# A new order of the first key, query and weight units in an attention-and-Mish kernel planned by hand

## The chip, the cores and the metric

The kernel runs on one core of one Trainium2 chip. The metric is the device time of one execution in microseconds. Before the change it is 1046.02 us, the median of three runs (1045.72 to 1046.89).

## The reference, cut to what matters

Two blocks follow each other, all in float32. The first is a linear attention with random features, for 8 batches, 8 heads, 576 positions and 64 dimensions per head:

```python
def phi(x):
    proj = np.einsum('bhsd,df->bhsf', x, w_phi)
    proj = proj - np.max(np.abs(proj), axis=-1, keepdims=True)
    return np.concatenate([np.exp(proj), np.exp(-proj)], axis=-1)
q_p, k_p = (phi(q), phi(k))
kv = np.einsum('bhsf,bhsd->bhfd', k_p, v)
z = np.sum(k_p, axis=2)
num = np.einsum('bhsf,bhfd->bhsd', q_p, kv)
den = np.einsum('bhsf,bhf->bhs', q_p, z)[..., None] + 1e-06
return (num / den).astype(np.float32)
```

The second takes the result as 4608 tokens of 512 numbers: `h = x @ w_in` (512 to 2048), `g = h * tanh(softplus(h))` (Mish), `g @ w_out` (2048 to 512).

## The kernel before, in words

Everything is cut into tasks. A class `Plan` receives each task with an engine, a key, an estimated duration, what it depends on and which buffers it takes and gives back. `Plan.order` walks through a modelled time: whenever an engine is free, it takes the ready task with the lowest key. The result is one fixed list, and on the chip each engine (TensorE or PE, VectorE or DVE, ScalarE or ACT, and SyncE or SP for DMA) works through its part of that list strictly in order. Keys are thus priorities, not times; a key that changes moves tasks in the queues of all four engines.

**Key units.** A key unit k0 to k35 is 512 positions of two heads each. `load_raw` (L352) fetches 256 KB; `project` (L360) multiplies by `w_phi` into two PSUM banks; `centre_max` (L364) takes the largest absolute value of each row on DVE, and `centre` (L372) subtracts it, also on DVE; `k_exp` (L436, L437) takes both exponentials on ACT, four activations of 128x512 for a unit; `k_sum` (L401) multiplies them with the values v (`load_v`, L431, 330 KB for a pair of heads). A pair of heads spans 4.5 tiles of 128 positions, so a sum runs over two units: k0 holds the first four tiles of pair 0, k1 the last one and four of pair 1, and so on. When a pair is complete, `kv_copy` takes its sum out of PSUM, on ACT (L469) if the pair is in `KVACT`, else on DVE (L471).

**Units in `BYACT`** take another way: DVE only finds the maximum (L392) and its negative (L395), and ACT computes the exponentials straight from PSUM with the maximum as its bias (L386), 16 activations of 128x128 in place of four of 128x512. Before the change these are k3 and k8.

**Query units.** q0_0, q0_1, q1_0, q1_1, q2_0, q2_1 are the first six (numbers 0 to 5 in `FIRST_QUERIES`): chunk c of 256 tokens, half g of the heads. They are projected and centred in the same way, turned by PE (`dt`, L480), go through ACT (L490), are multiplied with the sums (`num`, L401), divided on DVE (L523 to L525), turned again (`xt`, L545) and split into a high and a low part (`xTh` on ACT, L553; `xTl` on DVE, L559). A unit with g = 0 needs the sums of pairs 0 and 1, a unit with g = 1 those of pairs 2 and 3; pair 3 ends in k4.

**Weight units.** `w_in` and `w_out` lie in HBM as float64; 32 pieces of 512 KB each (in_0 to in_3 come first) are loaded as words (L251), most of them a second time shifted by two bytes ("middle", also L251), and turned into a high and a low float32 part by ACT (L265, L326) and six steps on DVE (L279, L284, L292, L297, L302, L307). There are three homes for middles, so the fourth middle waits until the first piece is split. `WKEYS` holds the keys of the 32 pieces.

**The second block.** The first matmuls of `h` (L575) need both halves of chunk 0 and the pieces in_0 to in_3; after that, `h` and `o` (L610) and, from chunk 4 on, a form with fewer products (L745) fill PE up to the end.

The order around the change is set by `FIRST_KEYS` and `FIRST_QUERIES` (the priority t of each early unit) and `WKEYS`. The priority of a load follows from t:

```python
load = (-40.0 + t if t < -3 else -46.6 + 0.2 * t) if first else t - 4.0
```

The words of weight piece i are loaded with key -47.5 + 0.1 i, its middle with -47.45 + 0.1 i. Of the first 11 loads in the list, those of v are moved back by about 4.5 places; four weight loads are moved behind the load of v5. All DMAs go through SP's one queue.

Of the kernel before, what the change touches and what calls it, by code (L numbers as in the profile page):

```python
# [33 lines left out]
PAIRED = 0  # L34
PSTEP = 1.0
NFLIGHT = 4
BYACT = (3, 8,)
KVACT = (0, 2, 3, 5, 6, 7,)
SLACK = -0.137
LAGF = 6  # L40
NMIX = 3
# [13 lines left out]

NK, LEAD = B * NHP * S // 512, 5
LEADIN = 5
FIRST_KEYS = {0: -15.83, 1: -13.11, 2: -9.97, 3: -9.13, 4: -7.79, 5: 5.39, 6: 7.33, 7: 10.36, 8: 12.26, 9: 26.17, 10: 26.27}
FIRST_QUERIES = {0: -11.55, 1: -8.5, 2: -1.4, 3: -0.74, 4: 12.74, 5: 12.11}
NFIRST = 6  # L60
NTRIAL = 3
NLOADS = 11
# [5 lines left out]
E1 = 0.171  # L68
GX = 0.403
ET = 0.107  # L70
WKEYS = [-6.42, -8.84, -5.8, -0.77, 4.55, 2.54, 6.13, 9.34, 4.27, 5.56, 11.66, 11.19, 18.21, 21.9, 23.26, 22.05,
         25.09, 22.07, 26.7, 34.84, 24.54, 37.47, 32.85, 40.81, 37.93, 41.3, 40.78, 41.2, 43.66, 37.64, 39.51, 45.36]
LAG, TAIL, TAILLAG = 4, 10, 2
TWOH = 10
HFIRST = 0.0
# [123 lines left out]
def attention_then_mish(ctx, tc, qT, kT, va, w_phi, w_in, w_out, out):  # L199
# [239 lines left out]
    def parts_of_unit(n):  # L439

        found = {}
        for i in range(4):
            for p, slot in pairs_of(4 * n + i):
                found.setdefault(p, []).append((i, slot))
        return found
# [16 lines left out]
    def kv_copy(p, more):  # L462
# [4 lines left out]
        kv[p // NHP, p % NHP] = work.tile([P, 2, 2, VW], F32, tag="kv", name=f"kv_{p}", bufs=NKV)  # L467
        if p in KVACT:
            nc.scalar.copy(kv[p // NHP, p % NHP], ps)  # L469
# [342 lines left out]
    add = plan.add  # L812
    key_time = dict(FIRST_KEYS)
    query_time = dict(FIRST_QUERIES)
    for n in range(NFIRST, 2 * NCH):
# [4 lines left out]
    def unit_tasks(unit, step, t, load, src, kinds, size):  # L820
# [12 lines left out]
        when = t - UCENTRE * (step >= NFIRST)  # L833
        if unit[0] == "k" and int(unit[1:]) in BYACT:
            add(f"centre {unit} 0", "DVE", t, 1.4, lambda: both_maxima(unit), deps=[f"project {unit}"])
# [23 lines left out]
    for t, is_query, n in units:  # L859
# [5 lines left out]
        if not is_query:  # L865
            unit = f"k{n}"
            kinds = ("h", "att") if n >= LEAD + TWOH else ("att", "att") if n % 2 or n >= LEADIN else ("h", "h")
            unit_tasks(unit, n - LEAD, t + 0.01 * steady, load, kT[n], kinds, 262144)
            for j in range(2):
                if n in BYACT:  # L870
                    home = e_homes_of[unit][j]
                    add(f"exp {unit} {j}", "ACT", exps[j], 1.75, lambda unit=unit, j=j, home=home: centred_exp(unit, j, home),
                        deps=[f"centre {unit} 0"], after=[f"exp {unit} 0"] if j else [], take=[(home, f"e{j}:{unit}")],
# [3 lines left out]
            mine = list(parts_of_unit(n).items())  # L877
            for k, (p, parts) in enumerate(mine):
                deps, take, give = [f"exp {unit} 0", f"exp {unit} 1"], [], []
                split, begins, ends, last = p >= SPLIT_PAIR, parts[0][1] == 0, parts[-1][1] == 4, k == len(mine) - 1  # L880
                bank_kind = "o" if p < NHP else "att"
                vslot = spare[NRAWSPARE // 2 + p] if p < NHP else "v"
                if begins:
                    add(f"load v{p}", "SP", load + 0.3, 0.42, lambda p=p: load_v(p), take=[(vslot, f"v:{p}")], size=337920,
                        after=turned_at(n - LEAD - 1))
                    deps.append(f"load v{p}")
                if begins or split:
                    take.append((bank_kind, f"kvps:{p}:{n if split else 0}"))
                if ends:
                    last_use.setdefault(vslot, []).append(f"sum {unit} {p}")  # L890
                    give.append(f"v:{p}")
                if last:
                    for h in e_homes_of[unit]:
                        last_use.setdefault(h, []).append(f"sum {unit} {p}")
                    give += [f"e{j}:{unit}" for j in range(2)]
                if steady:
                    sums_at.setdefault(n - LEAD, []).append(f"sum {unit} {p}")
                add(f"sum {unit} {p}", "PE", sums, 0.05 + 0.466 * len(parts), lambda n=n, p=p, last=last: k_sum(n, p, last),
                    deps=deps, after=[f"sum {unit} {mine[k - 1][0]}"] if k else [],
                    near=[f"exp q{(n - LEAD) // 2}_{(n - LEAD) % 2} {j}" for j in range(2)] if steady and n >= LEAD + 2 * NTURNED else [], take=take, give=give)  # L900
                if ends or split:
                    more = split and not begins
                    add(f"kv {p}" if ends else f"kv {p} first", "ACT" if p in KVACT else "DVE", sums + 0.01 - URGENT * steady, 0.34, lambda p=p, more=more: kv_copy(p, more),
                        deps=[f"sum {unit} {p}"] + ([f"kv {p} first"] if more else []), take=[] if more else [("kv", f"kv:{p}")],
                        give=[f"kvps:{p}:{n if split else 0}"])
        else:
            c, g = divmod(n, 2)
            unit = f"q{c}_{g}"
# [3 lines left out]
            for j in range(2):  # L912
                if by_dma:
# [6 lines left out]
                        deps=[f"turn {unit} {j}"], table="exp")  # L920
# [8 lines left out]
            for i in range(2):  # L929
                pair = 2 * g + i  # L930
                if steady:
                    sums_at.setdefault(n if is_query else n - LEAD, []).append(f"num {unit} {i}")
                add(f"num {unit} {i}", "PE", sums + 0.01, 0.95, lambda c=c, g=g, i=i: q_num(c, g, i),
                    deps=[f"exp {unit} 0", f"exp {unit} 1"] + [f"kv {b * NHP + pair}" for b in batches],
# [3 lines left out]
                    deps=[f"num {unit} {i}"], after=[f"divide {unit} 0"] if i else [], take=[] if i else [("half", f"x:{unit}")], give=[f"num{i}:{unit}"])  # L938
            outs = sums + GX if steady else t + 1.2
            if by_dma:  # L940
                add(f"regroup {unit}", "DVE", sums + 0.1, 0.68, lambda c=c, g=g: x_regroup(c, g),
                    deps=[f"divide {unit} {i}" for i in range(2)], take=[("part", f"via:{unit}")])
# [12 lines left out]
    for i, pc in enumerate(pieces):  # L955
# [4 lines left out]
            deps=last_use.get(slot, []) + used, after=ahead, take=[(slot, f"w:{nm}")], size=524288)  # L960
        if i < nmiddle:
            home = homes[i % len(homes)]
            add(f"middle {nm}", "SP", -47.45 + i * 0.1, 0.42, lambda pc=pc, home=home: load_middle(*pc, home),
                deps=last_use.get(home, []), take=[(home, f"m:{nm}")], size=524288)
        add(f"abs {nm}", "ACT", WKEYS[i] - 0.5, 0.55, lambda pc=pc: magnitude(*pc), deps=[f"load {nm}"], take=[("w", f"u:{nm}"), ("part", f"w:{nm}")])
        def split(step, took, fn, deps, **more):
            add(f"{step} {nm}", "DVE", WKEYS[i], took, lambda pc=pc, fn=fn: fn(pc), deps=deps, late=0.13, **more)

# [99 lines left out]
    for m in range(NFT // 2):  # L1068
        t = PREP + PSTEP * m
        for k in range(2):  # L1070
            add(f"wsum {m} {k}", "DVE", t, 0.61, lambda m=m, k=k: w_sum(m, k),
                deps=[f"{s} {('out', 2 * m + k, 0)}" for s in ("ready", "split")] + ([] if k else PREP_DEPS),
                after=[f"wsum {m} 0"] if k else [],
                take=[] if k else [("part", f"wsum0:{m}"), ("part", f"wsum1:{m}"), ("prep", f"prep:{m}")])
        for which in range(3):
# [3 lines left out]
                deps=[f"wsum {m} {k}" for k in range(2)], after=[f"comb {m} {which - 1}"] if which else [],  # L1079
# [3 lines left out]
                deps=[f"comb {m} {which}"])  # L1083
            add(f"combl {m} {which}", "DVE", t + 0.03 + 0.1 * which, 0.61 * width, lambda m=m, w=which: combine_low(m, w),
                deps=[f"combh {m} {which}"])
            for part in range(2):
                add(f"send {m} {which} {part}", "SP", t + 0.04 + 0.1 * which, 0.42, lambda m=m, w=which, p=part: combine_send(m, w, p),
                    deps=[f"combl {m} {which}"], size=int(262144 * width), give=held if part else [])
    for n in range(total):
        c, f = tiles[n]  # L1090
        deps = [f"{s} {('in', cc, f // 4)}" for cc in range(NCC) for s in ("ready", "split")] + [f"low q{c}_{g}" for g in range(2)]
# [14 lines left out]
        if f == end - 1:  # L1106
            continue
        when = n + 0.5 + LAG + min(max(0, n - total + TAIL), TAILLAG)
        deps = [f"low {c} {f // 2}"] + [f"{s} {('out', i, 0)}" for i in ((f - 1, f) if f == end else (f,)) for s in ("ready", "split")]
        gives = [f"g{f % 2}:{c}_{f // 2}"] + ([f"g{(f - 1) % 2}:{c}_{(f - 1) // 2}"] if f == end else [])  # L1110
        add(f"out {c} {f}", "PE", when, 2.82 if f == end else 1.41, lambda c=c, f=f: ff_out(c, f),
            deps=deps, after=[before_out] if before_out else [],
            take=[("o", f"o{tt}:{c}_{part}") for tt in range(2)] if f == first else [], give=gives)
        before_out = f"out {c} {f}"
        if f == end:
            for tt in range(2):
# [4 lines left out]
                else:  # L1121
                    take = [("half", f"osb{tt}:{c}")] if final else []
                add(f"evict {c} {f} {tt}", "ACT" if on_act else "DVE", when + 0.01, 0.6, lambda c=c, f=f, tt=tt: evict(c, f, tt),
                    deps=[before_out], take=take, give=[f"o{tt}:{c}_{part}"] + ([f"part{tt}:{c}"] if part and final else []))
# [43 lines left out]
```

## Time and profile before

| | |
|---|---|
| median of three runs | 1046.02 us |
| runs | 1046.02, 1046.89, 1045.72 us |
| span of the profiled execution, first to last instruction | 1043.5 us |
| PE busy | 1029.5 us (99%) |
| DVE busy | 738.0 us (71%) |
| ACT busy | 655.6 us (63%) |
| DMA | 223.09 MB, mean 214 GB/s |

The profile gives the profiled execution by its span alone; no separate time of that execution is listed. The three timed runs lie 2.2 to 3.4 us above the span, the median 2.5 us. Matmuls are pipelined and their ends are modelled, so PE's busy share is no measure of how near it is to its peak; its idle stretches are real. "Issue" in a wait or a chain means that the engine waited for nothing the profile shows.

### The profile page before, as it was taken

The page shows a single profiled execution, that of the slowest core. Times are in us where ns is not written, and L with a number is a line of the kernel's source. Part 1 is how long each engine was busy: PE and PEld are TensorE (multiplying, and loading weights), DVE is VectorE, ACT ScalarE, POOL GpSimd, SP SyncE. Part 2 cuts the span into 40 slices and gives each one's busy share as a digit, 9 for nine tenths or more (in the row PEclk, how much of TensorE's full clock was granted, in tenths as well). Part 3 has the DMA queues.
Part 4 walks back from the last instruction along what each step waited for, and adds up shares of the span by engine and source line. Part 5 has one row for each costly group of instructions (what it writes and reads, how often), then busy time and mean ns, then how long its engine had stood idle before and what let it go on. Part 6 is the DMA issues. An engine that isn't in the chain of part 4 may idle for free.

```text
span 1043.5 us, 30075 instructions
## 1 busy us (share of the span) xinstructions
PE 1029.5 (99%) x12286; PEld 990.6 (95%) x12286; DVE 738.0 (71%) x1692; ACT 655.6 (63%) x1028; POOL 0.7 (0%) x6
## 2 busy tenths in 40 slices
PE   8999999999999999999999999999999999999998
PEld 7888998899889999999999999999999999999998
DVE  7998998677886675767676767675776666666553
ACT  6799898667665756666666656665665565545532
POOL 0000000000000000000000000000000000000000
PEclk9999999999999999999999999999999999999999
DMA  9768664465977666767667564757576666765844
GB/s 319 271 235 317 189 209 136 125 204 160 296 246 235 212 211 205 222 215 226 216 209 230 193 209 159 242 186 243 175 237 196 206 189 212 219 220 190 291 142 155
DMA packets 158313, 223.09 MB, mean 214 GB/s; under 512 B 17120, under 2 KB 75616, under 8 KB 158176
## 3 DMA queue, kind: packets, MB, share of 16 engines
q1 hardware_dynamic: 158032, 221.11, 64.8%
q8 instruction: 97, 1.59, 0.6%
q14 instruction: 40, 0.33, 0.1%
q10 hardware_dynamic: 144, 0.07, 0.0%
HBM read 177.59 MB, written 43.52 MB: 212 GB/s over the span
## 4 chain that ended last, share of the span: by engine, by line
PE 93%; DVE 3%; DMA 3%; issue 1%; SPq 1%; ACT 0%; DVEq 0%; ACTq 0%
PE h L575 38%; PE oy L745 8%; PE ox L745 8%; PE o L610 8%; PE ow L745 8%; PE num L401 7%; PE kvps L401 6%; PE oz L745 4%; PE pp_q L360 4%; PE pp_k L360 3%; DMA middle_in<-w_in 1%; DMA words_out<-w_out 1%; DMA v<-va 1%; DMA words_in<-w_in 0%; PE dt L480 0%
## 5 line engine op out<-in xcount | busy, mean ns | idle before, releaser
L575 PE MATMUL h<-xTh,win 128*128 128x256 f32 x2304 | 429.1, 280 | 1.0 <-DVE e_k L372 1.0
L575 PEld LDWEIGHTS h<-xTh,win 128*128 128x128 f32 x2304 | 361.0, 188 | 5.2 <-PE h L575 1.2
L575 PE MATMUL h<-xTl,win 128*128 128x256 f32 x1152 | 321.9, 279 | 0.0
L575 PEld LDWEIGHTS h<-xTl,win 128*128 128x128 f32 x1152 | 216.5, 188 | 1.8
L660 DVE TENSOR_TENSOR sl<-s,sh 128x640 fp32r<-128x640 f32 x112 | 92.0, 823 | 106.7 <-ACT sh L656 101.7
L656 ACT CAST sh<-s 128x640 fp32r<-128x640 f32 x112 | 80.7, 722 | 90.8 <-DVE s L651 79.2
L641 ACT ACTIVATE u<-h 128x512 f32<-128x512 f32 x112 | 66.9, 598 | 96.2 <-PE h L575 95.7
L649 DVE TENSOR_TENSOR s<-u 128x256 f32<-128x256 f32 x112 | 46.9, 418 | 90.5 <-ACT u L641 90.3
L401 PEld LDWEIGHTS kvps<-v,e_k 128*64 128x64 f32 x2560 | 78.4, 137 | 9.4 <-issue 4.2
L401 PE MATMUL kvps<-v,e_k 128*64 128x66 f32 x2560 | 84.0, 223 | 3.2 <-issue 2.5
L745 PE MATMUL oy<-wout,sh 128*128 128x256 f32 x448 | 85.7, 284 | 0.0
L745 PE MATMUL ox<-wout,gh 128*128 128x256 f32 x440 | 83.6, 283 | 0.0
L745 PE MATMUL ow<-wout,sh 128*128 128x256 f32 x440 | 82.9, 281 | 0.0
L610 PE MATMUL o<-wout,gh 128*128 128x512 f32 x256 | 81.7, 400 | 0.0
L401 PE MATMUL num<-kv,e_q 128*64 128x66 f32 x2304 | 78.1, 225 | 1.8 <-DVE xTl L559 1.0
L401 PEld LDWEIGHTS num<-kv,e_q 128*64 128x64 f32 x2304 | 73.2, 139 | 4.9 <-issue 1.5
L436 ACT ACT_TABLE_LOAD x25 | 32.1, 1283 | 64.9 <-DVE e_k L372 64.5
L745 PEld LDWEIGHTS oy<-wout,sh 128*128 128x128 f32 x448 | 68.5, 188 | 1.6
L745 PEld LDWEIGHTS ox<-wout,gh 128*128 128x128 f32 x440 | 67.2, 188 | 0.7
L745 PEld LDWEIGHTS ow<-wout,sh 128*128 128x128 f32 x440 | 67.4, 188 | 0.0
L745 PE MATMUL oy<-wout,sl 128*128 128x256 f32 x224 | 62.9, 281 | 0.0
L745 PE MATMUL ow<-wout,sl 128*128 128x256 f32 x220 | 61.7, 280 | 0.0
(120 smaller groups left out, 1824.4 us busy)
## 6 DMA issues: line engine op xcount, KB each, us to landing
wout<-terms SPq DMA_DIRECT2D x344, 256.0 KB, 4.6
there_e<-e_q SPq DMA_DIRECT2D x60, 256.0 KB, 2.6
e_q<-there_e SPq DMA_DIRECT2D x240, 64.0 KB, 2.3
v<-va SPq DMA_DIRECT2D x32, 330.0 KB, 4.8
out<-osb SPq DMA_DIRECT2D x35, 256.0 KB, 2.6
raw_k<-kT SPq DMA_DIRECT2D x34, 256.0 KB, 3.5
raw_q<-qT SPq DMA_DIRECT2D x34, 256.0 KB, 3.5
there_x<-via SPq DMA_DIRECT2D x30, 256.0 KB, 2.0
```

The lines of the kernel that those rows point to most:

```text
L360: nc.tensor.matmul(ps[j][:, n], raw[rows, n * P:(n + 1) * P], w_phi2[rows], start=True, stop=True)
L401: nc.tensor.matmul(ps[rows], lhsT[h], rhs[h], start=start, stop=stop, skip_group_check=True)
L436: nc.scalar.activation(e[:, 1, :], e[:, 0, :], AF.Exp)
L575: nc.tensor.matmul(ps, w[:, wcol], x[:, cc % 2, :], start=(n == 0), stop=(n == 11))
L610: nc.tensor.matmul(ps.rearrange("p (k n) -> p k n", k=2), g[:, cols], w, start=(i == first and k == 0), stop=(i == end and k == 2))
L641: nc.scalar.activation(u, h_live.pop((c, fp)).rearrange("p f s -> p (f s)"), AF.Mish)
L649: nc.vector.tensor_tensor(s[:, :CH], u[:, :CH], u[:, CH:], op=ALU.add)
L656: nc.scalar.copy(mix_high[c, fp], mixed[c, fp])
L660: nc.vector.tensor_sub(mix_low[c, fp], mixed.pop((c, fp)), mix_high[c, fp].bitcast(F32))
L745: nc.tensor.matmul(ps, a, b, start=(begins and n == 0 and (apart or not half)), stop=(ends and n == 2), skip_group_check=True)
```

## The change

Eleven priorities of key units, six of query units and 32 of weight pieces get new values; k9 and k10 replace k8 among the units whose maximum is ACT's bias (k3 stays); pairs 1, 8, 9 and 10 of the sums go from DVE to ACT, pairs 5 and 6 from ACT to DVE; and the sum of a unit that continues a pair is listed only after the previous unit's sum of that pair.

```diff
-BYACT = (3, 8,)
-KVACT = (0, 2, 3, 5, 6, 7,)
+BYACT = (3, 9, 10,)
+KVACT = (0, 1, 2, 3, 7, 8, 9, 10,)
-FIRST_KEYS = {0: -15.83, 1: -13.11, 2: -9.97, 3: -9.13, 4: -7.79, 5: 5.39, 6: 7.33, 7: 10.36, 8: 12.26, 9: 26.17, 10: 26.27}
-FIRST_QUERIES = {0: -11.55, 1: -8.5, 2: -1.4, 3: -0.74, 4: 12.74, 5: 12.11}
+FIRST_KEYS = {0: -28.37, 1: -21.13, 2: -11.28, 3: -9.04, 4: -7.25, 5: 4.51, 6: 8.2, 7: 8.99, 8: 13.7, 9: 23.15, 10: 27.59}
+FIRST_QUERIES = {0: -19.3, 1: -3, 2: -8.37, 3: -2.04, 4: 9.1, 5: 12.34}
-WKEYS = [-6.42, -8.84, -5.8, -0.77, 4.55, 2.54, 6.13, 9.34, 4.27, 5.56, 11.66, 11.19, 18.21, 21.9, 23.26, 22.05,
-         25.09, 22.07, 26.7, 34.84, 24.54, 37.47, 32.85, 40.81, 37.93, 41.3, 40.78, 41.2, 43.66, 37.64, 39.51, 45.36]
+WKEYS = [-1.84, -10.76, -14.13, -2.86, 5.57, 0.84, 7.07, 7.43, 2.41, 6.16, 16.14, 7.86, 20.96, 22.8, 24.89, 22.26,
+         26.69, 16.44, 27.65, 26.37, 6.33, 38.3, 28.71, 36.83, 39.02, 43.27, 40.18, 42.34, 46.46, 28.96, 31.91, 45.62]
...
-                    deps=deps, after=[f"sum {unit} {mine[k - 1][0]}"] if k else [],
+                    deps=deps, after=([f"sum {unit} {mine[k - 1][0]}"] if k else []) + ([] if begins else [f"sum k{n - 1} {p}"]),
```

## Rows read from the trace of the kernel before

**Rows 1.** The page's list of engines: busy us, share of span, instructions.
```profile
PE 1029.5 (99%) x12286; PEld 990.6 (95%) x12286; DVE 738.0 (71%) x1692; ACT 655.6 (63%) x1028; POOL 0.7 (0%) x6
```

**Rows 2.** Busy time by stretch: length; PE, PEld, DVE, ACT, POOL; PE clock, DMA, GB/s.
```profile
5.20:20.00 14.80, 13.41 (x248) 12.55 (x250) 13.15 (x25) 9.40 (x17) 0.00 (x0) 1.00 1.03 370
20.00:36.70 16.70, 15.09 (x386) 13.88 (x382) 15.12 (x36) 13.71 (x35) 0.00 (x0) 1.00 0.80 270
36.70:44.80 8.10, 5.88 (x85) 5.27 (x81) 7.93 (x22) 4.90 (x9) 0.00 (x0) 0.79 1.02 391
...
67.00:83.00 16.00, 14.21 (x207) 11.71 (x203) 15.06 (x33) 15.01 (x26) 0.00 (x0) 1.00 0.92 316
83.00:200.00 117.00, 117.00 (x1209) 105.80 (x1210) 102.84 (x233) 97.10 (x163) 0.00 (x0) 1.00 0.58 194
...
290.00:345.00 55.00, 53.63 (x659) 51.52 (x659) 39.57 (x90) 33.48 (x52) 0.00 (x0) 1.00 0.70 228
```

**Rows 3.** PE's waits over the whole span: us in total, times, longest.
```profile
PE kvps L401 <- issue: 2.5, 2, 1.6
...
PE xt L545 <- DVE x L525: 1.2, 1, 1.2
...
PE num L401 <- DVE xTl L559: 1.0, 1, 1.0
...
PE kvps L401 <- DMA v<-va: 0.7, 1, 0.7
```

**Rows 4.** PE alone from 41 to 42 us: length, busy (matmuls), granted clock, DMA, GB/s.
```profile
41.00:42.00 1.00, 1.00 (x22) 0.50 1.08 397
```

**Rows 5.** The chain that ended last: start us, us, what.
```profile
40.68 3.74 PE num L401 x64
...
48.69 2.02 PE num L401 x64
```

**Rows 6.** DVE's waits, the first from 5.2 to 20 us, the second from 20 to 45 us.
```profile
DVE middle_in L284 <- DMA middle_in<-w_in: 1.5, 1, 1.5
...
DVE r L523 <- PE num L401: 1.4, 2, 1.1
```

**Rows 7.** The order of work before the first h: start us, us, engine, line, operation.
```profile
26.69 0.97 PEld L360 LDWEIGHTS pp_k<-w_phi,raw_k 64*128 64x128 f32 x16 [0.17 <-issue]
...
39.01 0.42 DVE L284 TENSOR_SCALAR middle_in<-middle_in 128x512 uint32<-128x512 uint32 x1
...
43.27 0.68 DVE L307 SCALAR_TENSOR_TENSOR win<-middle_in 128x512 fp32r<-128x512 uint32 x1
...
44.76 0.36 PE L575 MATMUL h<-xTh,win 128*128 128x256 f32 x1
```

**Rows 8.** SP's queue: DMA issues; the wait there; middles in halves, KB each, us to landing.
```profile
28.02 0.80 SPq L251 DMA_DIRECT2D middle_in<-w_in  x2
...
SPq L251 <- DVE win L307: 4.9, 1, 4.9
...
middle_in<-w_in SPq DMA_DIRECT2D x8, 255.8 KB, 6.1
```

**Rows 9.** DVE's and ACT's groups up to 200 us; last, L386's durations and starts.
```profile
L372 DVE TENSOR_TENSOR e_k<-pp_k,m_k 128x512 f32<-128x512 f32 x22 | 14.1, 682 | 0.0
L471 DVE COPY kv<-kvps 128x264 f32<-128x264 f32 x4 | 1.7, 427 | 0.7 <-PE kvps L401 0.7
L395 DVE TENSOR_SCALAR mm_k<-mm_k 128x4 f32<-128x4 f32 x4 | 0.6, 165 | 0.0
...
L436 ACT ACTIVATE e_k<-e_k 128x512 f32<-128x512 f32 x22 | 13.8, 626 | 6.2 <-DVE e_k L372 6.2
L386 ACT ACTIVATE e_k<-pp_k,mm_k 128x128 f32<-128x128 f32 x32 | 8.5, 427 | 0.0
L469 ACT COPY kv<-kvps 128x264 f32<-128x264 f32 x6 | 2.3, 377 | 0.0
...
L386 ACT ACTIVATE e_k<-pp_k,mm_k x32: 350/427/503, 21.2 to 100.2; 128x128 f32<-128x128 f32 x32
```

## The prediction

> **What bounds the kernel now.** The page's list of engines comes first: PE is busy for 99% of the span, DVE for 71%, ACT for 63% [rows 1]. So the time is PE's work, which the change leaves as it is, plus the stretches in which PE has nothing to do or runs slowly; only these can be won, and only new ones lost. The table by stretch shows where they are [rows 2]: PE idles 1.4 us from 5.2 to 20 us, 1.6 us from 20 to 36.7, 2.2 us (8.10 less 5.88) from 36.7 to 44.8, 1.8 us from 67 to 83, nothing from 83 to 200, and 1.4 us from 290 to 345. That is 8.4 us in all, 0.8% of the time.
>
> PE's waits say what ended them [rows 3]. 2.5 us, in two stops of the key sums, are "issue": no engine and no transfer that the profile shows was late. 1.2 us and 1.0 us wait for DVE (a division, then the low part of a query), and 0.7 us for a load of v. The two waits for DVE lie in the stretch from 36.7 to 44.8, just ahead of the first matmuls of h, and they cost more than their length. PE is busy 5.88 of 8.10 us there [rows 2], and from 41 to 42 us the granted clock is 0.50, the 1.2 GHz level [rows 4]. The 64 matmuls of a numerator that run there take 3.74 us on the chain, against 2.02 us for the same 64 a little later [rows 5]: 1.7 us more, which no list of waits shows.
>
> Why is DVE late there? From 5.2 to 44.8 us it is busy 13.15 + 15.12 + 7.93 = 36.2 of 39.6 us [rows 2], so before the first h it is DVE, not PE, that sets the pace, and its own idle time counts one for one. It has two larger waits: 1.5 us for the middle of the first weight piece, and 1.4 us for numerators [rows 6]. Its last task for the first h, the low part of in_3, starts at 43.27, and the first h at 44.76 [rows 7]; the task stands behind the centring of q1_1, which this h does not need yet.
>
> **The change part by part.**
>
> *Loads.* The DMA engines are full from 5.2 to 20 us (share 1.03), at 370 GB/s [rows 2], so a load is moved by the bytes ahead of it. Counting in the code: the middle of in_0 has had 4466 KB issued up to its end before, 3880 KB after, since k4 and the fourth pair of v now come behind it. 586 KB at 370 GB/s are 1.6 us, which covers DVE's wait of 1.5 us for it [rows 6]. q1_0 takes the place of q0_1 and lands as early as that did; it needs only pairs 0 and 1, so DVE and PE have its work while k4 and q0_1 come. k4 pays: 5672 KB stand up to its end, 2452 KB before, and 3220 KB at 370 GB/s are an estimated 8.9 us later. Before, by the same rate, k4 lands some 7 us behind the first issue, but is projected only at 26.69 [rows 7]; 8.9 us fit into that slack. I cost the moved loads at nothing beyond the gain on DVE. What covers k4 is PE's list; were k4 projected as soon as it landed, its delay would be paid in full.
>
> *Order on DVE.* in_3 (-2.86) now goes ahead of q1_1's centring (-2.04); before it was about level with it. That centring, by the code's own figure 2.4 us, comes off the way to in_3's end. The wait for numerators (1.4 us) hangs on PE, whose stop at "issue" precedes it; I let half of it stay.
>
> *Copies.* Pair 1 leaves DVE before the first h: 0.43 us [rows 9]. Together DVE reaches the end of in_3 sooner by 1.5 + 0.7 + 0.4 = 2.6 us without its reordering, and by up to 5 with it. PE's loss in the stretch that this relieves is 2.2 us of idle time and 1.7 us of half clock, so 3.9 us is all that can come back there, however early DVE is. I take 2.2 + 1.7 = 3.9. The bounds are 3.9 gained and, if the new list makes PE wait twice as long in that stretch, 3.9 lost.
>
> *Clock.* The row gives 0.50 [rows 4] in the stretch in which PE is thinnest [rows 2]. The Trainium skill (TensorE: Matmul & The Clock Gate, Part 1) states that the throttled level is the default and that activity releases it; by that rule the 1.7 us go with the idle time, and come back with any other stretch as thin. The trace agrees in this one place. If the clock fell anyway, the term would be 2.2 in place of 3.9.
>
> *The bias form.* For a unit that joins, DVE saves two subtractions of 0.682 us and adds two steps of 0.165 us: 1.0 us. ACT has 16 activations, 8.5 us for the 32 of two units, so 4.25 us, in place of four of 0.626 us, 2.5 us: 1.7 us more [rows 9]. The copies of pairs 5 and 6 go to DVE, 0.85 us, and fall into the stretch from 67 to 83, where DVE is busy 15.06 of 16 us [rows 2] and has 0.9 us free; I put 0.3 us of them on PE, between 0 (they fit) and 0.85 (none does). k8's activations start no later than 100.2 and are the last of the two units' [rows 9], so k8's return to DVE lies behind 83 us, as do k9, k10 and pairs 8 to 10. There DVE gets 1.0 us and gives 2.0 + 1.3 us, ACT gets 3.4 + 1.1 us and gives 1.7. PE has no wait from 83 to 200 us, and ACT is busy 97.10 of 117 us [rows 2], so this costs nothing; if that cover goes, ACT's 2.8 us more are the price.
>
> *Stops at "issue" and later waits.* Nothing in the change takes away the 2.5 us of "issue" [rows 3]: at nothing, between all of it gained and as much lost. The 1.4 us from 290 to 345 belong to a list that is planned anew; at nothing, between 1.4 gained and 1.4 lost. The added ordering of sums only repeats what the sums' lists did, as far as the units come in number order, which their keys do: nothing.
>
> Sum: -3.9 + 0.3 = -3.6 us. The profiled execution's span is 1043.5 us and the median of the runs is 1046.02, 2.5 us above; I take the difference over unchanged: **1042.4 us**.
>
> **The rivals.** *The waiting moves on (no change).* PE would come to the stretch from 67 to 83 us 3.9 us sooner, DVE, by its own saved idle time and the copy, only 2.6. DVE is busy 15.06 of 16 us there and has 0.85 us more to do, so PE would wait 1.3 + 0.85 = 2.2 us there for what it gained: -1.7 us, 1044.3; with the 0.7 us of numerator waits kept as well, 1045.0. For it speaks how full DVE is; against it that behind 83 us DVE and ACT never hold PE up, at 88% and 83% busy, so that PE must have work listed that needs neither.
>
> *in_0 is split last (slower).* in_0's key falls from -6.42 to -1.84, behind all of the first nine units and three other pieces. The fourth middle, in_3's, waits for the home that in_0 frees: before, SP waits 4.9 us for that split and issues the middle at 28.02 [rows 8], and everything queued in SP behind it (k5, the next v, more weight pieces) waits too. DVE first touches that middle at 39.01 [rows 7], by when it has had 11 us; the median transfer of half a middle takes 6.1 [rows 8], so 5 us are free. It decides from a split of in_0 at 33 us on. If it came at the very end, with q1_1's centring and the steps of in_1, in_2 (2.6 us each by the durations in the code) ahead of it, it would be some 8 us later, so h 3 us later, and PE's thin stretch would last longer at half clock: +3 us, 1049. Against it speaks that in_0 still lands first, so that DVE can use it whenever nothing else is ready.
>
> *More than forecast.* If the list also takes away the wait for v (0.7 us), the rest of the idle time from 67 to 83 (1.1 us) and half of the "issue" stops (1.2 us), the gain is 3.9 + 3.0 - 0.3 = 6.6 us: 1039.4. That needs three unrelated places to come out well.
>
> *The change does little of what it says.* Where the greedy list finds only one ready task, keys decide nothing; the loads could move and DVE's order stay. That leaves 0.4 us of the copy and 1.5 us of the middle, less 0.3: -1.6, 1044.4, which counts with the unchanged.
>
> **How the numbers follow.** A measurement of this kernel can tell some 0.2%, 2.1 us, from no change, so "faster" begins below 1043.9. The forecast has 0.43, more than forecast 0.17: together 0.60 faster. The waiting that moves on (0.15) and the change that does little (0.09) make 0.24 unchanged. in_0 split last has 0.16: slower. The range leaves out about half of the last and a little below the best: 1038.8 to 1048.0. It takes in the bounds of "issue" (2.5) below and the twofold wait, in part, above.
>
> **What would show it.** In the changed profile: DVE without its wait for the middle of in_0; the first h ahead of 43 us in place of 44.8; a granted clock of 1.00 throughout 36 to 46 us and 64 numerator matmuls at 2.0 us there; "issue" stops of the same count. PE idle from 67 to 83 near 2.1 us. Wrong would be: the clock at 0.50 in another early stretch; SP waiting longer than 4.9 us for a split; a PE wait for ACT behind 83 us, where ACT now has more; or a first h that is as late as before though DVE no longer waits, which would put the pace with PE's list or the loads.

## The result, and the profile after

The changed kernel takes 1052.68 us (median of 4 runs, 1050.13 to 1053.12), the kernel before beside it 1045.87 us (4 runs, 1043.78 to 1046.89). The ratio is 1.0067, with a 95% interval of 1.0052 to 1.0081: slower by some 7 us, where 3.6 us less were forecast. The profiled execution took 1050.13 us with a span of 1048.3 us, 4.8 us above the span of before. It is the fastest of the four; the median lies 2.5 us above it, and what makes those 2.5 us stands in no trace.

The page's list of engines, against [rows 1]:

```profile
PE 1032.8 (99%) x12286; PEld 990.2 (94%) x12286; DVE 736.7 (70%) x1690; ACT 660.3 (63%) x1044; POOL 0.7 (0%) x6
```

PE has as many matmuls as before, ACT 4.7 us more work, DVE 1.3 us less. Busy time by stretch, with the columns of [rows 2]:

```profile
5.20:20.00 14.80, 12.03 (x236) 10.61 (x234) 13.63 (x27) 9.65 (x18) 0.00 (x0) 1.00 1.03 365
20.00:36.70 16.70, 16.55 (x392) 14.93 (x392) 15.99 (x39) 14.54 (x37) 0.00 (x0) 1.00 0.88 295
36.70:44.80 8.10, 7.14 (x135) 5.80 (x135) 7.31 (x20) 5.96 (x13) 0.00 (x0) 1.00 0.96 364
...
67.00:83.00 16.00, 15.08 (x154) 12.25 (x154) 15.67 (x34) 13.58 (x23) 0.00 (x0) 1.00 0.91 302
83.00:200.00 117.00, 116.05 (x1246) 104.48 (x1246) 98.02 (x221) 100.35 (x175) 0.00 (x0) 1.00 0.53 181
290.00:345.00 55.00, 51.58 (x626) 49.66 (x621) 41.74 (x95) 36.23 (x54) 0.00 (x0) 0.97 0.72 229
```

The thin stretch has filled up: PE is busy 7.14 of 8.10 us from 36.7 to 44.8, in place of 5.88, at a clock of 1.00. At first sight the first 83 us look better. But PE idles 2.8 us from 5.2 to 20, 0.95 us from 83 to 200, where it idled nothing, and 3.4 us from 290 to 345, where the clock is now the one that falls. The change names nothing that works as late as that: its last weight piece starts its last step at 172.4 us.

Busy time hides a low clock and matmuls that are late by little, so I count **PE's loss** as well: the distance from each matmul's start to the next one's, less the usual distance of its kind in these traces (117 ns for `h`, 235 for `o`, 117.6 for its form with fewer products, L745, 31.5 for the sums and numerators, 68 for projections, 110 for turns), summed by stretch. The columns are one profiled execution each; kernels other than the first two are told below.

```
us          before  after  before_k7  after_again  exp_late  kv8_dve  after_both
0-83         14.68  12.83    12.66       15.27       13.19     12.68     12.55
83-290        1.52   2.68     1.66        2.76        2.72      1.55      1.54
290-345       2.79   6.14     3.28        4.18        4.05      3.76      3.97
345-end       7.65   9.75     8.67        9.13        8.42      9.34      8.87
sum          26.64  31.40    26.27       31.35       28.37     27.34     26.93
span        1043.5 1048.3   1043.2      1048.2      1045.3    1044.2    1043.8
```

The sum of loss rises by 4.76 us from before to after, and the span by 4.8: for these two executions the table accounts for the whole of it. It is -1.85 in front, +1.16 up to 290, +3.35 from 290 to 345, +2.1 behind.

**From 290 to 345 us.** PE's waits in the changed kernel, first of 85 to 200 us, then of 200 to 345 (us in total, times, longest):

```profile
PE pp_k L360 <- ACT kv L469: 0.9, 1, 0.9
...
PE h L575 <- ACT u L641: 2.0, 1, 2.0
PE h L575 <- DVE e_k L372: 0.9, 1, 0.9
```

The wait of 0.9 us for a centring was there before too (a loss of 1.16 us at 302 us). The one of 2.0 us for `u` is new. `u` is ACT's exponential in the Mish of chunk 4; it frees the PSUM bank that the next `h` needs. ACT's order of work there, in the changed kernel (start us, us, engine, line, operation):

```profile
303.06 1.28 ACT L436 ACT_TABLE_LOAD   x1 [1.25 <-DVE e_k L372]
304.36 0.64 ACT L436 ACTIVATE e_k<-e_k 128x512 f32<-128x512 f32 x1
305.02 0.63 ACT L437 ACTIVATE e_k<-e_k 128x512 f32<-128x512 f32 x1
...
306.29 1.28 ACT L641 ACT_TABLE_LOAD   x1
307.58 0.60 ACT L641 ACTIVATE u<-h 128x512 f32<-128x512 f32 x1
...
309.57 1.28 ACT L436 ACT_TABLE_LOAD   x1
```

and in the kernel before:

```profile
301.72 0.73 ACT L656 CAST sh<-s 128x640 fp32r<-128x640 f32 x1 [3.61 <-DVE s L651]
302.66 0.60 ACT L641 ACTIVATE u<-h 128x512 f32<-128x512 f32 x1 [0.22 <-PE h L575]
...
303.71 1.28 ACT L436 ACT_TABLE_LOAD   x1
```

Before, ACT takes the Mish exponential that is due first (302.66), then loads the other table once for all four exponentials of k16. After, the first two exponentials of k16 come ahead: ACT waits 1.25 us for DVE, loads their table, computes them, and loads the table of `u` again. `u` comes at 307.58 in place of 302.66. And then the clock, in PE's stretches (length, busy, clock, DMA, GB/s):

```profile
306.00:307.00 1.00, 0.20 (x2) 1.00 0.78 264
307.00:308.00 1.00, 0.00 (x0) 1.00 0.78 293
...
311.00:312.00 1.00, 1.00 (x6) 0.50 0.91 298
313.00:314.00 1.00, 1.00 (x11) 1.00 0.50 142
```

PE stands for 1.8 of 2 us, and from 309.0 on the granted clock is 0.50, the 1.2 GHz level, for 3.4 us: 1.7 us more. That is the same pair of a wait and its clock that I had read at 41 us of before.

**From 83 to 200 us**, the wait for `kv`. Pair 8's copy is one of those that went to ACT:

```profile
159.90 1.28 ACT L581 ACT_TABLE_LOAD   x1
161.20 0.60 ACT L581 ACTIVATE u<-h 128x512 f32<-128x512 f32 x1
...
162.44 0.37 ACT L469 COPY kv<-kvps 128x264 f32<-128x264 f32 x1
```

It stands behind a table load and a Mish on ACT, and PE waits for its PSUM bank.

**The first 83 us.** DVE's and PE's waits of the changed kernel, from 5.2 to 45 and from 5.2 to 83 us, against [rows 3, 6]:

```profile
DVE middle_in L284 <- DMA middle_in<-w_in: 1.2, 3, 0.6
...
DVE r L523 <- PE num L401: 0.4, 1, 0.4
```

```profile
PE num L401 <- ACT e_q L490: 1.4, 2, 1.2
...
PE pp_q L360 <- ACT win L326: 0.8, 1, 0.8
PE num L401 <- issue: 0.5, 1, 0.5
PE h L575 <- DVE xTl L559: 0.4, 1, 0.4
...
PE kvps L401 <- issue: 0.2, 1, 0.2
PE xt L545 <- DVE x L525: 0.2, 1, 0.2
```

DVE's waits for numerators went from 1.4 to 0.4 us, PE's waits for `x` from 1.2 to 0.2 and for `xTl` from 1.0 to 0.4. In their place stand 1.2 us for ACT's `e_q` near 19 us and 0.8 for ACT's `win` at 68. The first `h` starts at 45.60, later than at 44.76 [rows 7]. No wait stands ahead of it; PE comes to it from its own numerators:

```profile
43.92 1.74 PE L401 MATMUL num<-kv,e_q 128*64 128x66 f32 x52 [0.15 <-ACT e_q L490]
45.60 0.39 PE L575 MATMUL h<-xTh,win 128*128 128x256 f32 x1
```

DVE is late by then all the same. Its order of work, with SP's (SPq):

```profile
37.28 0.68 DVE L307 SCALAR_TENSOR_TENSOR win<-middle_in 128x512 fp32r<-128x512 uint32 x1
...
38.50 1.27 SPq L251 DMA_DIRECT2D middle_in<-w_in  x1
...
44.43 0.43 DVE L284 TENSOR_SCALAR middle_in<-middle_in 128x512 uint32<-128x512 uint32 x1 [0.65 <-DMA middle_in<-w_in]
...
45.71 0.69 DVE L307 SCALAR_TENSOR_TENSOR win<-middle_in 128x512 fp32r<-128x512 uint32 x1
```

The first line is the end of in_0's split, at 37.96; in_1 and in_2 were done nine microseconds before it. Only then is the home free for in_3's middle: issued at 38.50 where it was 28.02 [rows 8], and DVE waits 0.65 us for it at 44.43. The `xTl` for which PE waits 0.4 us, a few matmuls into the first `h`, stands behind that split on DVE. This is what the rival "in_0 is split last" said would happen, though without its price, as will be seen.

### The profile page after: what moved, and what is told of

The parts are those of the page before. It is cut to its first block, busy times and chain, and to the rows that moved or that the text cites. A ratio compares the mean times of both kernels' runs of the same rounds, so it can differ in the third digit from the quotient of the medians.

```text
span 1048.3 us, 30080 instructions
## 1 busy us (share of the span) xinstructions
PE 1032.8 (99%) x12286; PEld 990.2 (94%) x12286; DVE 736.7 (70%) x1690; ACT 660.3 (63%) x1044; POOL 0.7 (0%) x6
## 4 chain that ended last, share of the span: by engine, by line
PE 87%; DVE 4%; ACT 4%; DMA 4%; SPq 1%; issue 1%; ACTq 0%
PE h L575 35%; PE oy L745 8%; PE ox L745 8%; PE ow L745 7%; PE o L610 7%; PE num L401 6%; PE kvps L401 6%; PE oz L745 4%; PE pp_q L360 3%; PE pp_k L360 3%; DMA middle_in<-w_in 1%; DMA wout<-terms 1%; DMA words_in<-w_in 1%; DMA raw_k<-qT 1%; DMA e_q<-there_e 1%
## 5 line engine op out<-in xcount | busy, mean ns | idle before, releaser
L745 PE MATMUL oy<-wout,sh 128*128 128x256 f32 x448 | 85.6, 284 | 0.0
L745 PE MATMUL ox<-wout,gh 128*128 128x256 f32 x440 | 84.1, 283 | 0.1
L745 PE MATMUL ow<-wout,sh 128*128 128x256 f32 x440 | 83.0, 281 | 0.0
L745 PEld LDWEIGHTS oy<-wout,sh 128*128 128x128 f32 x448 | 68.5, 188 | 1.6
L745 PEld LDWEIGHTS ox<-wout,gh 128*128 128x128 f32 x440 | 67.2, 188 | 1.5 <-DMA wout<-terms 0.7
L745 PEld LDWEIGHTS ow<-wout,sh 128*128 128x128 f32 x440 | 67.4, 188 | 0.2 <-DMA wout<-terms 0.2
L745 PE MATMUL oy<-wout,sl 128*128 128x256 f32 x224 | 62.8, 281 | 0.0
L745 PE MATMUL ow<-wout,sl 128*128 128x256 f32 x220 | 61.7, 280 | 0.0
```

The costliest lines, as they stand in the source:

```text
L745: nc.tensor.matmul(ps, a, b, start=(begins and n == 0 and (apart or not half)), stop=(ends and n == 2), skip_group_check=True)
```

## The experiments

Three theories stood first. A: ACT has too much work (the units in `BYACT`, the copies). B: the new order of the weight pieces does it. C: no one part does it; the list as a whole falls badly at places that nobody chose.

**The parts, undone or alone.** The ACT part of the change taken back in the changed kernel:

```diff
-BYACT = (3, 9, 10,)
-KVACT = (0, 1, 2, 3, 7, 8, 9, 10,)
+BYACT = (3, 8,)
+KVACT = (0, 2, 3, 5, 6, 7,)
```

> The changed kernel with both engine choices put back: k3 and k8 in the bias form, pairs 0, 2, 3, 5, 6, 7 copied by ACT; the new order of units and weight pieces stays. Theory A (ACT's added work of 83 to 200 us, some 3 us busy, delays the high parts that DVE waits for, so that DVE's sums of weights slip behind 290 us and PE waits there): PE's loss from 290 to 345 us falls from 3.4 to about 1.4 us idle and the half clock there goes; ratio to before about 0.998. Theory B (the new order of weight pieces alone moves those sums): as slow as the changed kernel, ratio 1.006 to 1.007, PE idle 3 us or more from 290 to 345. Theory C (no part owns it; each new list meets chunk 4 by chance): anything, without relation to ACT's busy time.

Measured: 1056.67 us, 1.0118 [1.0105, 1.0131] of before. Slower still. The same lines the other way, the ACT part alone put into the kernel before:

> The kernel before with the two engine choices of the change alone (k3, k9, k10 in the bias form; pairs 0 to 3 and 7 to 10 copied by ACT). Theory A: slower by most of the loss, ratio 1.004 to 1.008, with PE waiting for ACT behind 83 us and idle more than 2.5 us from 290 to 345. Theory B: ratio within 0.002 of 1. Theory C: unlike either side in sign and place.

Measured: 1046.98 us, 1.0029 [1.0016, 1.0042]. The weights' keys taken back in the changed kernel:

```diff
-WKEYS = [-1.84, -10.76, -14.13, -2.86, 5.57, 0.84, 7.07, 7.43, 2.41, 6.16, 16.14, 7.86, 20.96, 22.8, 24.89, 22.26,
+WKEYS = [-6.42, -8.84, -5.8, -0.77, 4.55, 2.54, 6.13, 9.34, 4.27, 5.56, 11.66, 11.19, 18.21, 21.9, 23.26, 22.05,
...
```

> The changed kernel with the 32 weight priorities of before. Theory A: as slow as the changed kernel, ratio 1.005 to 1.008, and PE idle about 3 us from 290 to 345. Theory B: ratio about 0.998, loss from 290 to 345 as in the kernel before (1.4 us idle).

Measured: 1055.41 us, 1.0106 [1.0092, 1.0121]. And the priorities of the key and query units, with the ordering of sums, alone in the kernel before:

```diff
-FIRST_QUERIES = {0: -11.55, 1: -8.5, 2: -1.4, 3: -0.74, 4: 12.74, 5: 12.11}
+FIRST_QUERIES = {0: -19.3, 1: -3, 2: -8.37, 3: -2.04, 4: 9.1, 5: 12.34}
...
```

> The kernel before with the new priorities of the first key and query units alone (and the added order of sums). Both A and B: the first 83 us gain 1 to 4 us (no half clock at 41 us), nothing is lost later: ratio 0.996 to 0.999. Theory C: the early gain stands, but the stretch from 290 to 345 moves by 1 to 4 us either way.

Measured: 1053.13 us, 1.0077 [1.0063, 1.0090].

A and B fall: if either part were the cause, taking it back would bring time back, and both cost time. Nor do the parts add up. In each of the four kernels PE has new waits, and each time others (with the ACT part alone 2.3 us for DVE's `e_q` and 1.2 for ACT's `u`). PE's waits with the ACT part undone, then with the weights undone, then with the units alone:

```profile
PE h L575 <- DVE e_q L372: 3.0, 1, 3.0
```

```profile
PE h L575 <- ACT u L581: 3.7, 1, 3.7
...
PE h L575 <- ACT u L641: 2.3, 1, 2.3
```

```profile
PE pp_k L360 <- DVE e_k L372: 3.1, 2, 2.8
...
PE h L575 <- DVE e_q L372: 1.8, 1, 1.8
```

The waits of 3.0 us (at 195 us) and 3.7 us (at 189) each come with 6.8 us at clock 0.50. So theory C is left: what an edit costs is the cost of the list that comes out.

**How little it takes.** If C holds, an edit of next to no content should move the time as well. One key of a query unit, and one of a key unit, each moved by 0.16 in the kernel before:

```diff
-FIRST_QUERIES = {0: -11.55, 1: -8.5, 2: -1.4, 3: -0.74, 4: 12.74, 5: 12.11}
+FIRST_QUERIES = {0: -11.55, 1: -8.5, 2: -1.4, 3: -0.9, 4: 12.74, 5: 12.11}
```

> The kernel before with a single priority changed, that of q1_1 from -0.74 to -0.9, which puts it ahead of in_3 (-0.77) where both are ready. Theory C (every new list places its PE waits anew, over the whole front and the start of chunk 4, and a small edit is enough): slower by 3 to 12 us, with new waits of 1 to 4 us far from the edit, behind 150 us. Against it (what an edit costs lies where the edit is): within 3 us, and all of the difference ahead of 60 us.

Measured: 1058.63 us, 1.0136 [1.0122, 1.0150], the slowest of all, and more than the 3 to 12 us of theory C. By the count of the table it loses 12.4 us up to 83 us, no more than before, but 10.1 up to 290 and 7.9 up to 345. PE's waits from 83 to 345 us:

```profile
PE h L575 <- ACT u L581: 3.5, 3, 1.7
...
PE pp_q L360 <- DVE kv L465: 1.9, 2, 1.7
...
PE pp_q L360 <- ACT u L641: 1.8, 1, 1.8
```

Which order of tasks makes each of these waits was not tested.

k7's key from 10.36 to 10.2:

```diff
-FIRST_KEYS = {... 7: 10.36, ...}
+FIRST_KEYS = {... 7: 10.2, ...}
```

> The kernel before with k7's priority 10.2 in place of 10.36, an edit as small as that of q1_1. Theory C (an edit costs what the new list happens to hold, not what its size suggests): here the list changes little and the start of chunk 4 keeps its order, so within 0.002 of 1, either way.

Measured: 1044.79 us, 1.0000 [0.9990, 1.0010]. A small edit can cost 14 us or nothing. The two do not do the same to the list, though. The key of q1_1 passes that of in_3, and the order of work in the traces differs from 35 us on, on DVE first and from 55 us on all four engines. The key of k7 passes no other key of the three tables, and the order differs only between 79 and 103 us; behind that it is that of before. The second kernel serves as a control as well: up to 79 us its order of work is that of before, yet in its profiled execution the clock did not fall at 41 us, though PE is as thin there (busy 5.54 of 8.10 us) and waits the same 1.2 us for `x` and 1.0 for `xTl`:

```profile
36.70:44.80 8.10, 5.54 (x91) 4.81 (x90) 7.89 (x21) 5.63 (x11) 0.00 (x0) 1.00 1.03 373
```

Its loss up to 83 us is 12.66 us, that of the changed kernel 12.83.

**The place at 305 us.** Now single tasks are moved in the finished list, so that nothing else is planned anew. In the changed kernel, k16's first exponential goes back behind the Mish, to just before its second:

```diff
+        name = [task["name"] for task in tasks].index
+        task = tasks.pop(name("exp k16 0"))
+        tasks.insert(name("exp k16 1"), task)
```

> The changed kernel's list with one task moved: on ACT, the first half of k16's exponentials goes behind the Mish of the second and third pair of chunk 4, as its second half does; nothing else moves. Theory D (in the changed list ACT meets k16 before that Mish, loads the table of exp and loads Mish's again, and h's bank comes back 3 to 5 us late): PE's wait of 2.0 us for u goes, two table loads fewer, no half clock near 309 us; loss from 290 to 345 falls from 6.1 to about 2.8 us; 2 to 4 us less than the changed kernel, ratio to before 1.003 to 1.005. Theory E (DVE's late sums of weights hold that stretch up, whatever ACT's order): PE waits there for DVE in place of ACT, gain under 1 us, ratio 1.006 or more.

Measured: 1048.90 us, 1.0040 [1.0026, 1.0055]. ACT's order of work, then PE's waits from 83 to 345 us:

```profile
305.45 0.59 ACT L645 ACTIVATE u<-h 128x512 f32<-128x512 f32 x1
...
307.44 1.28 ACT L440 ACT_TABLE_LOAD   x1
```

```profile
PE h L579 <- ACT u L645: 0.5, 1, 0.5
...
PE oz L749 <- DVE osb L632: 0.7, 1, 0.7
```

The wait for `u` falls from 2.0 to 0.5 us, and a wait of 0.7 us for DVE's `osb` (its copy of an `o` out of PSUM) comes that was not there. The stretch from 290 to 345 loses 4.05 us, in place of the 2.8 expected. That is 2.1 us less than the 6.14 of the changed kernel, but 1.7 of these are the half clock. In the repeat of the changed kernel, told below, PE has the same wait without a fall of the clock:

```profile
PE h L575 <- ACT u L641: 2.1, 1, 2.1
...
310.00:315.00 5.00, 4.67 (x40) 4.67 (x41) 3.44 (x11) 4.87 (x9) 0.00 (x0) 1.00 0.75 242
```

There the stretch loses 4.18 us, and with pair 8's copy put back, again with the wait and without a fall, 3.76. With the task moved, five profiles lose 3.0 to 4.05. So at full clock the moved task gives back little in this stretch, 0.3 us between the averages, which the spread of single executions covers; what it takes away is chiefly the fall of the clock. What else is in the 0.23% between the two ratios stays open.

The reverse edit in the kernel before: the first half of k16's exponentials goes ahead of the Mish of the second pair, the second half behind that of the third:

```diff
+        task = tasks.pop(name("exp k16 0"))
+        tasks.insert(name("mixh 4 0"), task)
+        task = tasks.pop(name("exp k16 1"))
+        tasks.insert(name("mish 4 2") + 1, task)
```

> The kernel before with the reverse edit alone: the first half of k16's exponentials goes ahead of the Mish of chunk 4's second pair, the second half behind the third's. Theory D: two table loads more, PE waits 2 to 3 us for u near 305 us, a half clock may follow; 2 to 5 us slower, ratio 1.002 to 1.005. Theory E: within 0.001 of 1.

Measured: 1046.67 us, 1.0019 [1.0006, 1.0032]. ACT's order of work and PE's wait in it:

```profile
301.30 1.28 ACT L442 ACT_TABLE_LOAD   x1 [5.45 <-DVE e_k L378]
...
305.81 0.60 ACT L647 ACTIVATE u<-h 128x512 f32<-128x512 f32 x1
```

```profile
PE h L581 <- ACT u L647: 2.1, 1, 2.1
```

The wait of 2.1 us is made out of nothing but the order of these tasks, the half clock follows at 307.6 us, and the loss from 290 to 345 is 5.95 us, as in the changed kernel (6.14). That ACT's order makes the wait is shown from both sides. What the wait costs is not one number: of the 3 us more in this profile 1.7 are the half clock.

**Pair 8's copy**, put back on DVE in the changed kernel:

```diff
-        if p in KVACT:
+        if p in KVACT and p != 8:
```

> The changed kernel's list with the copy of pair 8 given to DVE at its place in the list (ACT otherwise makes it behind a Mish and its casts). If the engine choice makes the wait of 0.9 us at 162 us: the wait goes, 0.5 to 1 us less than the changed kernel (ratio 1.005 to 1.006). If PE's lead over both engines makes it, it turns into a wait for DVE of like length, no gain.

Measured: 1048.52 us, 1.0036 [1.0023, 1.0048]. The wait for `kv` is gone, and the loss from 83 to 290 falls from 2.68 to 1.55 us. By the ratios the time fell by some 2.8 us, more than this 1.1 and more than the 0.5 to 1 us expected. The profiled execution, the fastest of the ten, has no fall of the clock at 309 us; where the rest of the gain came from, it does not show.

**Both edits together**, beside the changed kernel once more, and before:

> The changed kernel as it is, beside the next three on one chip, so that what the two moved tasks give can be read without a change of chip. Ratio to before 1.005 to 1.008; a granted clock below 1.00 in most executions (PE's wait of 2 us near 306 us is followed by a stretch at the lower level).

Measured: 1050.83 us, 1.0063 [1.0050, 1.0076], beside 1044.5 us for before (26 runs).

> The changed kernel's list with both edits: k16's first half behind the Mish of chunk 4, and pair 8 copied by DVE. Theory D, with the front costing the same in both kernels: 3 to 5 us less than the changed kernel, ratio to before 0.999 to 1.002, and PE's loss within 1 us of the kernel before in every stretch but those that differ by a half clock. If the front of the changed list were really better by 2 us or more (the prediction's mechanism): ratio 0.996 to 0.998. If something else in the changed list costs: ratio 1.003 or more.

Measured: 1047.67 us, 1.0028 [1.0016, 1.0040]. The two edits give back 3.2 us of 6.3. By themselves they gave 0.23% and 0.27%, together 0.35%; with intervals of 0.12 to 0.15% to either side that is not told from their sum. The interval shuts out a front that is better by 2 us (ratio 0.998 or less); it does not decide between theory D (1.002 or less) and something else that costs (1.003 or more).

**A task moved in before.** The combinations of chunk 7 and their sends, which DVE and SP do just ahead of k16's centring, moved behind it:

```diff
+        late = ["combl 7 1", "combl 7 2", "send 7 1 0", "send 7 1 1", "send 7 2 0", "send 7 2 1"]
...
+        at = 1 + [task["name"] for task in tasks].index("centre k16 0")
+        tasks[at:at] = held
```

> The kernel before with the two low parts of the last weight sums (and their four sends) moved behind k16's centring on DVE, which the matmuls of h wait 1.0 us for near 303 us. If DVE's order there makes that wait: 0.5 to 1 us faster, ratio 0.999 to 0.9995, which may not be told from 1. If the wait is that of the PSUM bank alone: unchanged.

Measured: 1045.19 us, 1.0001 [0.9987, 1.0015]. The gain did not come: the wait for `e_k` went, and PE waits 1.0 us for `u` in the same place. One wait covers the other.

**What is left of the 0.28%.** Three more traced executions of the kernel with both edits (theories F and G are those of all three; the expectation of the first is given), and one of before:

> The changed kernel with both moved tasks, for another trace. Theory F (what is left, 0.28%, is in waits for loads around 68 us and the falls of the clock behind them, which vary from one execution to the next): PE's loss from 67 to 83 us is 1.4 to 4 us, more than the 1 to 1.8 of the kernel before at full clock, the other stretches are equal within 0.5 us. Theory G (it is spread over the steady part): the loss behind 345 us is 1 us or more above that of the kernel before, 4.9 to 5.4.

> The kernel before once more, for a trace on the same chip: the first 83 us lose 12.5 to 13.2 us without a fall of the clock, 14.5 to 15 with one (at 41 us); behind 345 us 4.9 to 5.5.

Measured: 1047.51, 1046.10 and 1047.25 us, and before 1045.11 and, without a trace, 1046.16. The loss behind 345 us is 9.10, 8.96 and 9.20 us, against 7.65 and 7.87 in two executions of before (the figure for before in the expectation is too low; this is the count as in the table): some 1.3 us more, as theory G had it, in a kernel whose edits lie far ahead. In each of the three PE waits 0.3 to 0.4 us for the landing of a piece of `wout`, between 344 and 347 us; in the traces of before it does not. From 290 to 345 the three lose 3.0 to 3.9 us against 2.8 to 2.95, mostly the wait for `osb`. Together that is 1.3 + 0.6 = 1.9 of some 3 us. Up to 83 us they lose 12.9 to 14.7 us, before 14.0 and 14.7, so nothing of the rest is shown to lie there, against theory F; it stays open. So does the cause behind 345 us: the kernel with k7's key moved, which works there in the order of before and is as fast, loses 8.67 us, so that 1 us can come from the execution alone. No kernel that ran was faster than the one before.

## Why the prediction was wrong

**What bounds the kernel** was read rightly: PE's work stays, and only its stretches of waiting or low clock move the time. All that the profiled pair differs by is PE's loss, to 0.1 us.

**The term of 3.9 us, the step "I take 2.2 + 1.7 = 3.9".** It failed in two ways. First, the 1.7 us of half clock at 41 us belong to a part of the executions, not to the kernel: of five profiles with the front of before, three have this fall, and in the kernel with k7's key moved PE is as thin and the clock stays at 1.00. Of 59 executions of the kernel before in three series of runs, 36 had a mean clock of 0.999 or 1.00, which leaves no room for 3.4 us at 0.50 (0.16% of the span), with medians of 1043.8, 1044.1 and 1044.2 us in the series; 23 were below, with medians of 1045.2, 1045.8 and 1045.5. So only in part of its runs was there a fall to win back. Second, the idle time did not vanish, it moved on: against the k7 kernel, whose clock did not fall either, the changed one loses 1.9 us less from 20 to 36.7 us (1.43 for 3.30), and more in every other stretch of the front, 2.95 to 3.52, 1.94 to 2.24, 1.75 to 2.30 and 0.98 to 1.43, with the waits for ACT's `e_q` and `win` that took the place of those for DVE.

The premise that DVE sets the pace up to the first `h` does not hold in the rows of before either. DVE had ended the split of in_3 at 43.95, and PE came to the `h` at 44.76 [rows 7] from its own numerators, 40.68 to 44.42 [rows 5], and turns:

```profile
44.35 0.66 PE L480 MATMUL dt<-ident,e_q 128*128 128x128 f32 x4
```

What the step had right is the place. With the changed front PE is busy 6.9 to 7.3 of the 8.1 us there in all eight profiles, where it was busy 5.5 to 6.4 in the five with the front of before, and in none of the eight does the clock fall there; in two of them it falls at 70 us. But the first 83 us lose as much: 12.7 to 14.7 us with the front of before, 13.5 on the average, and 12.6 to 15.3 with the changed one, 13.6 on the average. The term measured is zero, and the 1.85 us gained in the profiled pair are the luck of which execution was profiled. The rule that I set beside the trace, that activity releases the clock (the Trainium skill, TensorE: Matmul & The Clock Gate, Part 1), would have given the 1.7 us back; the runs agree only so far that each fall in the traces follows a wait or a thin stretch of PE, and do not show that each such stretch brings a fall.

**Loads.** The middle of in_0 no longer costs 1.5 us, as forecast, but DVE waits for middles in three places still, 1.2 us in all. in_3's is one of them.

**Copies and the bias form.** PE's idle time from 67 to 83 is 0.9 us, less than the 2.1 that I put there; the copies of pairs 5 and 6 cost nothing to be seen. ACT's 2.8 us more "cost nothing" behind 83 us: wrong for pair 8. The step took a mean of 117 us (ACT busy 97 of 117) for a place: one copy of 0.37 us came to stand behind a table load and a Mish, 2.5 us from the one's start to its own, and PE waited 0.9.

**From 290 to 345 us at nothing, between -1.4 and +1.4.** This step failed as well: +3.35 in the profiled pair, outside the bounds, and in the repeat, where the clock did not fall at that place, +1.4, at the bound. With the front at nothing, it is this stretch, the one from 83 to 290 (+1.2 in both) and the one behind 345 that turn the sign. I took the idle time of the list of before as the measure for another list. What belonged there was the price of the narrow place: a PSUM bank that returns late by a table load of 1.28 us, two exponentials, another table load and a wait, some 4.9 us in ACT's order, of which PE's own list covers all but 2.0; and 1.7 more where the clock falls. The trace of before holds all of these durations.

**Behind 345 us** I had no term at all; +2.1 us in the profiled pair, +1.5 in the repeat, and some 1.3 us in the three further traces of the kernel with both edits. Its cause is open.

**The rivals.** "In_0 is split last" came true in its mechanism, even beyond its threshold (the split ended at 37.96, the threshold was 33), and in_3's middle came late by it. Its price of 3 us did not come: PE had sums and numerators to do, waited 0.4 us for the `xTl` behind that split, and the first 83 us lose no more than before. It is right in sign for a reason that it did not name. The wait by which it was to be known, SP's for a split, did not grow either (4.1 us, for 4.9). "The waiting moves on" describes the first 83 us best, though not at the place that it named: PE's idle time from 67 to 83 fell.

**What would show it.** Of the five signs, the clock at 1.00 from 36 to 46 us came, and DVE's wait for the middle of in_0 fell from 1.5 to 0.3 us; but the k7 kernel shows the clock at 1.00 there without the change. Of those that were to prove it wrong two did, a PE wait for ACT behind 83 us and a first `h` no earlier; a third, the clock at 0.50 in another early stretch, came in the repeat, at 70 us. "Issue" stops went from 2.5 to 0.7 us in this profile, and are 1.5 and 0.7 us for two groups in the k7 kernel's: they vary by execution, and no run ties them to the change.

## What to carry to other kernels

Where a planner writes one in-order list for all engines, an edit at the front prices the whole list: a key moved by 0.16, past another key, cost 14 us, and one moved as far, past none, nothing. So compare the two lists first, and look for the narrow places of the whole span before costing the edit (a bank that comes back behind a table switch, a copy behind a long activation), bound them by those prices and not by the idle time of the old list, and when one is found, move single tasks in the finished list, which tests it alone. A half clock seen in one profile is to be held against the clocks of many runs before it is counted as something to win.

## What the runs showed of the hardware

The same program falls to the 1.2 GHz level in some executions and not in others: 36 of 59 runs of before had a mean clock of 0.999 or 1.00, and the others took 1.3 to 1.7 us more by the medians of the three series. Of the ten runs of the changed kernel one had 0.999, the others 0.996 to 0.998. With the wait of 2.0 us for `u` cut to 0.5, four of six stayed at 1.00, and with both edits eight of nine at 0.999 or 1.00; with pair 8's copy alone put back, and the wait for `u` still 2.1 us, four of ten. These means do not say where in the span the clock fell. The wait makes a fall likely, but not sure: in the profiles of two kernels with that wait (the repeat, and pair 8 on DVE) the clock did not fall at that place. A stretch at 0.50 ahead of PE's last matmul lasted 3.4 or 6.8 us in every profile, and each came in or behind a stretch with a PE wait of 1 us or more; the k7 kernel has such waits, 1.2 us for `x` and 1.0 for `xTl`, without a fall.
